# A three-layer chain on one core: the single tile's 256-column groups put side by side into 512-column banks, and three second-layer groups moved into the next phase's first step

## The chip, the cores and the metric

The kernel runs on one core of a Trainium2 chip. Its time is device microseconds (us) of one execution. Engines are called PE (TensorE matmul, with PEld for its weight loads), DVE (VectorE), ACT (ScalarE), POOL (GpSimd) and SP (the engine that issues the DMAs). PSUM, into which PE writes, is used in banks of 128 partitions by 512 float32 columns.

## What is computed

A windowed attention on 4 x 576 tokens (8 heads of 64) gives x, 2304 tokens of 512 numbers. Two layers follow, both cut here to what matters:

```python
# mixture: 8 experts, P is a 2304 x 8 matrix from a softmax and 8 rounds of scaling
for e in range(8):
    out += P[:, e:e+1] * (np.maximum(x @ w1[e], 0) @ w2[e])      # 512 -> 1024 -> 512
# second layer, x is the out of the first
r = np.maximum(x @ w_in, 0)                                      # 512 -> 2048
return (r * r) @ w_out                                           # -> 512
```

## The kernel before

**Tokens.** The 2304 tokens are cut into two pairs of 1024 (tokens 0 to 1023 and 1280 to 2303) and one single tile of 256 (tokens 1024 to 1279). Attention takes the first part of the time; then 80 *steps* follow in four phases, one written after the other (`steps` and `first`, lines 458 to 461): 32 steps of the mixture for the first pair and the single tile (phase 0, steps 0 to 31), 32 for the second pair (phase 1, steps 32 to 63), 8 of the second layer for the first pair and the single tile (phase 2, steps 64 to 71), 8 for the second pair (phase 3, steps 72 to 79). A step takes 256 hidden columns of weights. Every product is done as three float32r matmuls (high by high, high by low part, low by high).

**First layer of a pair** (`l1_pair`, line 536): seven products u1 to u7 of 6 matmuls of 512 columns, a Strassen-like scheme, in PSUM tiles `s` (2 buffers), `xt` (2) and `pt` (1). u4, u5 and u6 all write the one `pt` bank: ACT copies it to `s2` after u4 (line 570) and to `s3` after u5 (line 574), and u5 and u6 wait for these copies. u3 writes again to the bank that ACT copies to `pt` after u1 (line 558).

**First layer of the single tile** (`l1_single`, line 591): two groups (fc 0 and 1) of 12 matmuls of 256 columns, each in half of a bank of its own (tile `mm`, 3 buffers).

**Evacuation** (`evac_g`, line 500): in the mixture from step 3 (`SCALED`) on, DVE makes g = max(z, 0) * p (line 525), ACT rounds it to the high part gh (line 533), DVE takes the low part gl = g - gh (line 511). In the second layer ACT makes max(z, 0) first (line 521). For the single tile p is the tile `ps` of 128 by 256, gh and gl are `sgh` and `sgl`, and each instruction takes 256 columns.

**Second layer** (`l2_units`, line 614): step i does it for the hidden columns of step i-1. The pair has 8 groups of 6 matmuls of 512 columns, which we call l2[0] to l2[7]. The single tile has in the mixture 4 groups of 6 matmuls of 256 columns (called s0 to s3 here), one for each 128 output rows, and in the second layer 2 groups of 512 columns. Each group takes a bank `mm`, and DVE adds the bank to an accumulator in SBUF (line 647). In the last step of a phase's sums the accumulator is stored to DRAM (lines 652 and 655, on SP).

**Order.** It is written out by hand, and each engine's queue is in this order. Within a step: u1 to u4, then l2[0], u5, l2[1], u6, l2[2], u7, then l2[3] to l2[7], then the single tile's second layer, then its first layer (lines 847 to 856). In the first step of a phase (32, 64, 72) all second-layer groups of the step before are run ahead of u1, and u1 to u7 follow each other with none between (lines 842 to 845). In step 64 the two first-layer groups of the single tile stand after u1 and u2 (line 854).

`after(k, f)` (line 484) puts the instructions of f behind the k-th unit from now; a unit is one of the groups above. So all work that is not a matmul has its place by a count of units. `prep_w` (line 123) so splits the next weights: POOL makes sums (lines 144 to 149), ACT rounds (line 131: `w2h` behind unit 1, `blkh` behind 2, `sumh` behind 10), DVE takes the low parts (line 135: `w2l` behind 3, `blkl` behind 5, `suml` behind 12), each no later than the step's last unit (line 858). `new_operands` (line 224) makes the seven operands x of a new phase: 12 pieces behind units 1 to 12 of the step before it and 12 behind units 14 to 25, counted from that step's start, so that the last of them run in the new phase's first step (POOL line 206, ACT line 209, DVE line 212). `narrow` (line 162) turns the second layer's weights from float64 to float32 in four stages; in phase 0 one stage stands behind units 0 and 8 of a step, so every second step has behind unit 8 the stage with three DVE instructions (lines 189 to 196).

```python
            order = l1[:4] if i else l1[2:4]
            for u in l1[4:]:
                order += l2[:1] + [u]
                l2 = l2[1:]
            order += l2 + l2s
```

Of the kernel before, what the change touches and what calls it, by code (L numbers as in the profile page):

```python
# [37 lines left out]
T = 512  # L38
# [9 lines left out]
def tile_kernel(ctx: ExitStack, tc: tile.TileContext, a):  # L48
# [37 lines left out]
    def bank(tag):  # L86
        return psum.tile([128, 512], F32, tag=tag, name=tag, bufs=bufs[tag])
# [163 lines left out]
    def spread(p, e, t0):  # L251
        n = p.shape[-1]
        c0, nch = t0 // 128, n // 128
        src = p_dram[c0:c0 + nch, e:e + 1, :].rearrange("c e n -> e c n")
        nc.sync.dma_start(p.rearrange("p (c n) -> p c n", n=128), src.to_broadcast([128, nch, 128]))
# [7 lines left out]

    def load_ps(e):
        if e < E:
            p = p_t[e] = post[0].tile([128, NSG], F32, tag="ps", name="ps", bufs=1)
            spread(p, e, SINGLE)

# [229 lines left out]
    def evac_g(i, ghi, glo, src, p, k):  # L500
# [21 lines left out]

        def product():
            held["g"] = tmp("g")[:, :n]
            nc.vector.scalar_tensor_tensor(  # L525
                out=held["g"], in0=src, scalar=0.0, in1=held["r"], op0=ALU.max, op1=ALU.mult
            )

        if not moe:
            after(k, square)  # L530
# [58 lines left out]
        return [u1, u2, u3, u4, u5, u6, u7]  # L589

    def l1_single(i):
        def unit(fc):
            if fc == 0:
                g_t[i, 1] = tuple(
                    post[0].tile([128, FC, NSG], F32R, tag=n, name=n, bufs=1) for n in ("sgh", "sgl")
                )
            gh, gl = g_t[i, 1]
            ps = bank("mm")[:, :NSG]
            hi, lo = wset[i % 2]["blk"]
            k = 0  # L600
            for kc in range(KC):
                c = slice((4 * fc + kc) * 128, (4 * fc + kc) * 128 + 128)
                for w, z in ((hi, xs_hi), (hi, xs_lo), (lo, xs_hi)):
                    nc.tensor.matmul(ps, w[:, c], z[:, kc], start=k == 0, stop=k == 3 * KC - 1)  # L604
                    k += 1
            p = p_t[steps[i][1] // SPE] if steps[i][0] and i >= SCALED else None
            evac_g(i, gh[:, fc], gl[:, fc], ps, p, 0)
            s = steps[i][1]
            if fc == FC - 1 and steps[i][0] and s % SPE == SPE - 1:
                after(1, lambda: load_ps(s // SPE + 1))  # L610

        return [lambda fc=fc: unit(fc) for fc in range(FC)]

    def l2_units(i, which):

# [9 lines left out]
        def unit(c, h, w):  # L625
# [20 lines left out]
            else:  # L646
                nc.vector.tensor_tensor(out=dst, in0=ps, in1=dst, op=ALU.add)  # L647
            if i == SCALED - 1:
                p = p_t[0] if which else p_t[0, 0, h // T]
                nc.gpsimd.tensor_tensor(out=dst, in0=dst, in1=p, op=ALU.mult)  # L650
            if last and moe:
                nc.sync.dma_start(y_dram[:, c, t0 + h:t0 + h + w], dst)
            elif last:
                ch = t0 // 128 + c
                nc.sync.dma_start(out[ch * 128:(ch + 1) * 128], dst)

        if moe:
            return [lambda c=c, h=h: unit(c, h, min(T, n)) for h in range(0, n, T) for c in range(KC)]
        return [lambda c=c: unit(c, 0, DM) for c in range(n // 128)]
# [15 lines left out]
    with tc.manual_schedule():  # L675
# [159 lines left out]
        for i in range(len(steps) + 1):  # L835
            l2 = l2_units(i - 1, 0)
            l2s = l2_units(i - 1, 1)
            if i == len(steps):
                for u in l2 + l2s:
                    run(u)  # L840
                break
            if i in first[1:]:
                for u in l2 + l2s:
                    run(u)
                l2, l2s = [], []
            l1 = l1_pair(i) if i else first_units
            order = l1[:4] if i else l1[2:4]
            for u in l1[4:]:
                order += l2[:1] + [u]
                l2 = l2[1:]  # L850
            order += l2 + l2s
            if i == first[2]:
                l1s = l1_single(i)
                order = l1[:1] + l1s[:1] + l1[1:2] + l1s[1:] + l1[2:]
            elif pair_of(i) == 0:
                order += l1_single(i)
            for k, f in prep_w(i):
                after(min(k, len(order) - 1), f)
            if i + 2 in first[1:]:
# [99 lines left out]
```

## Time and profile before

| | us |
|---|---|
| median of 3 runs (2043.14 to 2047.37) | 2044.98 |
| the profiled execution, its own time | 2052.68 |
| its span in the profile | 2050.9 |

The profile is of the one execution of 2052.68 us. All times of rows are microseconds from the start of its span, durations in us unless marked ns. In the timeline and in the chain, successive instructions that are alike are merged (x6 is six of them); `[0.17 <-DVE acc L647]` says that the engine stood idle for 0.17 us before this one and what ended the wait. L635 is line 635 of the kernel. Matmuls overlap: a matmul of 512 columns lasts some 0.39 us in the rows but the next starts 0.23 us after it; so a wait is read from start to start.

### The profile page before, as it was taken

What the parts mean: (1) busy time and instruction counts of PE and PEld (TensorE: products, weight loads), DVE (VectorE), ACT (ScalarE), POOL (GpSimd) and SP (SyncE); (2) the same over time, 40 slices, a digit from 0 to 9 for tenths busy, and PEclk for the clock granted to TensorE, in tenths of its full rate; (3) what the DMA queues carried; (4) which work ended last, traced back from release to release, by engine and by line L of the source; (5) the groups of instructions that cost most, each with busy time, mean ns of one, the idle gap of its engine ahead of it and who ended that gap; (6) DMA issues with size and microseconds to landing.
All of it is one profiled execution on the core that took longest, in us unless ns stands there. A gap on an engine that the chain in (4) does not pass through costs nothing.

```text
span 2050.9 us, 28660 instructions
## 1 busy us (share of the span) xinstructions
PE 2017.1 (98%) x11584; PEld 1663.0 (81%) x11584; DVE 1558.3 (76%) x2435; ACT 720.4 (35%) x1149; POOL 386.6 (19%) x416
## 2 busy tenths in 40 slices
PE   9999999999999999999999999999999999999999
PEld 7778888888888888888888888888888878887887
DVE  4766777777777777778888888888887786678676
ACT  3443222223322232223433333333333344344542
POOL 3522311111011111111311212121211231123120
PEclk8899999999999999999999999999999999999999
DMA  8512121222212121213222322323221231112111
GB/s 279 177 65 61 52 57 57 62 65 62 65 50 61 56 61 47 70 57 98 103 93 87 87 85 71 97 78 98 82 86 59 75 111 42 39 54 103 62 42 52
DMA packets 71509, 159.35 MB, mean 78 GB/s; under 512 B 6336, under 2 KB 33104, under 8 KB 71376
## 3 DMA queue, kind: packets, MB, share of 16 engines
q1 hardware_dynamic: 71376, 157.52, 23.8%
q8 instruction: 91, 1.49, 0.3%
q14 instruction: 42, 0.34, 0.1%
HBM read 137.49 MB, written 20.00 MB: 77 GB/s over the span
## 4 chain that ended last, share of the span: by engine, by line
PE 87%; DVE 10%; ACT 2%; issue 1%; POOL 0%; ACTq 0%; DVEq 0%; POOLq 0%
PE mm L635 42%; PE pt L477 16%; PE s L477 10%; PE xt L477 9%; PE mm L604 5%; DVE acc L647 3%; PE xt L349 2%; DVE gl L511 2%; DVE g L525 1%; DVE suml L135 1%; PE mm L752 1%; PE s L297 1%; PE pt L334 1%; DVE x_lo L212 1%; DVE s L584 1%
## 5 line engine op out<-in xcount | busy, mean ns | idle before, releaser
L647 DVE TENSOR_TENSOR acc<-mm,acc 128x512 f32<-128x512 f32 x746 | 473.2, 642 | 188.4 <-PE mm L635 184.4
L635 PE MATMUL mm<-gl,w2h 128*128 128x512 f32 x1024 | 403.3, 394 | 0.0
L635 PE MATMUL mm<-gh,w2h 128*128 128x512 f32 x1024 | 402.3, 393 | 0.8 <-DVE acc L647 0.7
L635 PE MATMUL mm<-gh,w2l 128*128 128x512 f32 x1024 | 402.8, 393 | 0.0
L533 ACT CAST gh<-g 128x512 fp32r<-128x512 f32 x308 | 191.5, 622 | 592.8 <-DVE g L525 592.6
L144 POOL TENSOR_TENSOR sums<-raw 128x256 f32<-128x256 f32 x80 | 66.2, 827 | 1466.7 <-DVE suml L135 1423.8
L635 PEld LDWEIGHTS mm<-gh,w2h 128*128 128x128 f32 x1024 | 192.4, 188 | 46.8 <-DVE acc L647 1.6
L635 PEld LDWEIGHTS mm<-gl,w2h 128*128 128x128 f32 x1024 | 192.3, 188 | 43.9
L635 PEld LDWEIGHTS mm<-gh,w2l 128*128 128x128 f32 x1024 | 192.3, 188 | 43.7
L511 DVE TENSOR_TENSOR gl<-g,gh 128x512 fp32r<-128x512 f32 x308 | 223.8, 731 | 0.9 <-ACT gh L533 0.9
L525 DVE SCALAR_TENSOR_TENSOR g<-s,pp 128x512 f32<-128x512 f32 x183 | 128.8, 704 | 111.6 <-PE s L477 109.4
L477 PE MATMUL pt<-x_hi,sumh 128*128 128x512 f32 x320 | 126.4, 395 | 3.7 <-ACT s L570 3.7
L477 PE MATMUL s<-x_hi,blkh 128*128 128x512 f32 x320 | 126.3, 395 | 1.0 <-ACT pt L558 1.0
L477 PE MATMUL xt<-x_hi,sumh 128*128 128x512 f32 x320 | 126.6, 396 | 0.0
L477 PE MATMUL xt<-x_lo,sumh 128*128 128x512 f32 x320 | 126.0, 394 | 0.0
L477 PE MATMUL pt<-x_lo,sumh 128*128 128x512 f32 x320 | 125.9, 393 | 0.0
L477 PE MATMUL xt<-x_hi,suml 128*128 128x512 f32 x320 | 125.9, 393 | 0.0
L477 PE MATMUL pt<-x_hi,suml 128*128 128x512 f32 x320 | 125.8, 393 | 0.0
L477 PE MATMUL s<-x_lo,blkh 128*128 128x512 f32 x320 | 125.8, 393 | 0.0
L477 PE MATMUL s<-x_hi,blkl 128*128 128x512 f32 x320 | 125.5, 392 | 0.0
L135 DVE TENSOR_TENSOR w2l<-raw,w2h 128x1024 fp32r<-128x1024 f32 x80 | 100.7, 1259 | 14.9 <-ACT w2h L131 14.9
L533 ACT CAST sgh<-g 128x256 fp32r<-128x256 f32 x74 | 29.9, 406 | 219.0 <-DVE g L525 219.0
(151 smaller groups left out, 3970.3 us busy)
## 6 DMA issues: line engine op xcount, KB each, us to landing
raw<-in_w SPq DMA_DIRECT2D x128, 512.0 KB, 3.5
raw<-w SPq DMA_DIRECT2D x32, 512.0 KB, 3.4
v<-in_v SPq DMA_DIRECT2D x24, 384.0 KB, 3.9
pp<-p_dram SPq DMA_DIRECT2D x32, 256.0 KB, 5.6
xb<-in_w_in SPq DMA_DIRECT2D x16, 512.0 KB, 4.7
w<-xb SPq DMA_DIRECT2D x32, 256.0 KB, 2.3
xb<-in_w_out SPq DMA_DIRECT2D x16, 512.0 KB, 4.7
k<-in_k SPq DMA_DIRECT2D x24, 224.0 KB, 4.6
```

The lines of the kernel that those rows point to most:

```text
L135: nc.vector.tensor_tensor(out=w[1], in0=src, in1=w[0].bitcast(F32), op=ALU.subtract)
L144: tt(out=c(sums, 0), in0=c(raw1, 2), in1=c(raw1, 3), op=ALU.add)
L212: return lambda: nc.vector.tensor_tensor(out=x_lo[:, k, j], in0=z, in1=x_hi[:, k, j].bitcast(F32), op=ALU.subtract)
L297: nc.tensor.matmul(ps[QB * head:QB * head + QB, 2 * (g % 3) + g // 3, :], qt[rows, pr, g * QB:g * QB + QB], kt[rows, pr, g * QB:g * QB + K ...
L349: nc.tensor.matmul(xt[D * h:D * h + D, pr, c * QB:c * QB + QB], vt[keys, c, head * D:head * D + D], pt[keys, c * 128 + head * QB:c * 128 + ...
L477: nc.tensor.matmul(ps, w[:, c], z[:, x, j], start=start and k == 0, stop=stop and k == 5, skip_group_check=True)
L511: nc.vector.tensor_tensor(out=glo, in0=z, in1=ghi.bitcast(F32), op=ALU.subtract)
L525: nc.vector.scalar_tensor_tensor(out=held["g"], in0=src, scalar=0.0, in1=held["r"], op0=ALU.max, op1=ALU.mult)
L533: after(k + 1, lambda: nc.scalar.copy(ghi, held["g"]))
L604: nc.tensor.matmul(ps, w[:, c], z[:, kc], start=k == 0, stop=k == 3 * KC - 1)
L635: nc.tensor.matmul(ps, lhsT, rhs, start=k == 0, stop=k == 3 * FC - 1)
L647: nc.vector.tensor_tensor(out=dst, in0=ps, in1=dst, op=ALU.add)
```

## The change

The single tile's first layer becomes one unit for steps from 3 on: both groups of 12 matmuls go into the two halves of one bank, and evacuation takes 512 columns at a time (the tile `ps` gets a middle dimension, so that it can be read twice over). In the mixture its second layer becomes two units (`unit_wide`) of 12 matmuls from step 4 on, each with two groups in one bank, one addition of 512 columns and in the last step one store. A step of phase 0 has then 18 units instead of 21, one of phase 2 18 instead of 19. In the first step of a phase the last three second-layer groups of the pair are kept back and stand before u5, u6 and u7 as in other steps; the other five and the single tile's run ahead as before. In step 64 the single tile's first-layer unit stands after u1.

```diff
--- before.py
+++ after.py
@@ -263,8 +263,8 @@
 
     def load_ps(e):
         if e < E:
-            p = p_t[e] = post[0].tile([128, NSG], F32, tag="ps", name="ps", bufs=1)
-            spread(p, e, SINGLE)
+            p = p_t[e] = post[0].tile([128, 1, NSG], F32, tag="ps", name="ps", bufs=1)
+            spread(p[:, 0, :], e, SINGLE)
 
 
 
@@ -522,9 +522,12 @@
 
         def product():
             held["g"] = tmp("g")[:, :n]
-            nc.vector.scalar_tensor_tensor(
-                out=held["g"], in0=src, scalar=0.0, in1=held["r"], op0=ALU.max, op1=ALU.mult
-            )
+            o, z, r = held["g"], src, held["r"]
+            if len(r.shape) == 3:
+                k = n // NSG
+                o, z = (y.rearrange("p (k n) -> p k n", k=k) for y in (o, z))
+                r = r.to_broadcast([128, k, NSG]) if k > 1 else r
+            nc.vector.scalar_tensor_tensor(out=o, in0=z, scalar=0.0, in1=r, op0=ALU.max, op1=ALU.mult)
 
         if not moe:
             after(k, square)
@@ -589,27 +592,34 @@
         return [u1, u2, u3, u4, u5, u6, u7]
 
     def l1_single(i):
-        def unit(fc):
-            if fc == 0:
+        def unit(fcs):
+
+            if fcs[0] == 0:
                 g_t[i, 1] = tuple(
                     post[0].tile([128, FC, NSG], F32R, tag=n, name=n, bufs=1) for n in ("sgh", "sgl")
                 )
             gh, gl = g_t[i, 1]
-            ps = bank("mm")[:, :NSG]
+            ps = bank("mm")[:, :len(fcs) * NSG]
             hi, lo = wset[i % 2]["blk"]
-            k = 0
-            for kc in range(KC):
-                c = slice((4 * fc + kc) * 128, (4 * fc + kc) * 128 + 128)
-                for w, z in ((hi, xs_hi), (hi, xs_lo), (lo, xs_hi)):
-                    nc.tensor.matmul(ps, w[:, c], z[:, kc], start=k == 0, stop=k == 3 * KC - 1)
-                    k += 1
+            for n, fc in enumerate(fcs):
+                k = 0
+                for kc in range(KC):
+                    c = slice((4 * fc + kc) * 128, (4 * fc + kc) * 128 + 128)
+                    for w, z in ((hi, xs_hi), (hi, xs_lo), (lo, xs_hi)):
+                        nc.tensor.matmul(
+                            ps[:, n * NSG:n * NSG + NSG], w[:, c], z[:, kc], start=k == 0, stop=k == 3 * KC - 1
+                        )
+                        k += 1
             p = p_t[steps[i][1] // SPE] if steps[i][0] and i >= SCALED else None
-            evac_g(i, gh[:, fc], gl[:, fc], ps, p, 0)
+            gh, gl = (g[:, fcs[0]:fcs[-1] + 1].rearrange("p f n -> p (f n)") for g in (gh, gl))
+            evac_g(i, gh, gl, ps, p, 0)
             s = steps[i][1]
-            if fc == FC - 1 and steps[i][0] and s % SPE == SPE - 1:
+            if fcs[-1] == FC - 1 and steps[i][0] and s % SPE == SPE - 1:
                 after(1, lambda: load_ps(s // SPE + 1))
 
-        return [lambda fc=fc: unit(fc) for fc in range(FC)]
+        if i >= SCALED:
+            return [lambda: unit(list(range(FC)))]
+        return [lambda fc=fc: unit([fc]) for fc in range(FC)]
 
     def l2_units(i, which):
 
@@ -646,7 +656,7 @@
             else:
                 nc.vector.tensor_tensor(out=dst, in0=ps, in1=dst, op=ALU.add)
             if i == SCALED - 1:
-                p = p_t[0] if which else p_t[0, 0, h // T]
+                p = p_t[0][:, 0, :] if which else p_t[0, 0, h // T]
                 nc.gpsimd.tensor_tensor(out=dst, in0=dst, in1=p, op=ALU.mult)
             if last and moe:
                 nc.sync.dma_start(y_dram[:, c, t0 + h:t0 + h + w], dst)
@@ -654,6 +664,28 @@
                 ch = t0 // 128 + c
                 nc.sync.dma_start(out[ch * 128:(ch + 1) * 128], dst)
 
+        def unit_wide(c):
+
+            ps = bank("mm")
+            for m in range(2):
+                k = 0
+                for fc in range(FC):
+                    for g, wt in ((gh, whi), (gl, whi), (gh, wlo)):
+                        nc.tensor.matmul(
+                            ps[:, m * NSG:m * NSG + NSG],
+                            wt[:, fc, (c + m) * 128:(c + m) * 128 + 128],
+                            g[:, fc],
+                            start=k == 0,
+                            stop=k == 3 * FC - 1,
+                        )
+                        k += 1
+            dst = acc[1][:, c * NSG:c * NSG + 2 * NSG]
+            nc.vector.tensor_tensor(out=dst, in0=ps, in1=dst, op=ALU.add)
+            if last:
+                nc.sync.dma_start(y_dram[:, c:c + 2, t0:t0 + NSG], dst.rearrange("p (c n) -> p c n", c=2))
+
+        if moe and which and i >= SCALED:
+            return [lambda c=c: unit_wide(c) for c in (0, 2)]
         if moe:
             return [lambda c=c, h=h: unit(c, h, min(T, n)) for h in range(0, n, T) for c in range(KC)]
         return [lambda c=c: unit(c, 0, DM) for c in range(n // 128)]
@@ -839,21 +871,21 @@
                 for u in l2 + l2s:
                     run(u)
                 break
+            ahead = []
             if i in first[1:]:
-                for u in l2 + l2s:
-                    run(u)
-                l2, l2s = [], []
+                ahead, l2, l2s = l2[:-3] + l2s, l2[-3:], []
             l1 = l1_pair(i) if i else first_units
             order = l1[:4] if i else l1[2:4]
+            l1s = l1_single(i) if pair_of(i) == 0 else []
+            if i == first[2]:
+                order = l1[:1] + l1s + l1[1:4]
+                l1s = []
             for u in l1[4:]:
                 order += l2[:1] + [u]
                 l2 = l2[1:]
-            order += l2 + l2s
-            if i == first[2]:
-                l1s = l1_single(i)
-                order = l1[:1] + l1s[:1] + l1[1:2] + l1s[1:] + l1[2:]
-            elif pair_of(i) == 0:
-                order += l1_single(i)
+            order += l2 + l2s + l1s
+            for u in ahead:
+                run(u)
             for k, f in prep_w(i):
                 after(min(k, len(order) - 1), f)
             if i + 2 in first[1:]:
```

## Rows read from the trace of the kernel before

**Rows 1.** The page, part 1: busy time of each engine, share of the span, instructions.
```profile
PE 2017.1 (98%) x11584; PEld 1663.0 (81%) x11584; DVE 1558.3 (76%) x2435; ACT 720.4 (35%) x1149; POOL 386.6 (19%) x416
```
**Rows 2.** Waits of PE, whole span: who waited for whom, us, times, longest.
```profile
PE mm L635 <- DVE acc L647: 11.3, 31, 1.4
```
**Rows 3.** Chain in order of time, first-layer groups of the single tile: start, us, what.
```profile
865.65 2.88 PE mm L604 x24
...
893.24 2.83 PE mm L604 x24
...
919.90 2.88 PE mm L604 x24
...
946.41 2.83 PE mm L604 x24
```
**Rows 4.** Timeline of PE in one step's tail: start, us, engine, line, operation.
```profile
346.58 0.28 PE L635 MATMUL mm<-sgh,w2h 128*128 128x256 f32 x1
...
347.62 0.39 PE L635 MATMUL mm<-sgh,w2h 128*128 128x256 f32 x1 [0.17 <-DVE acc L647]
...
348.98 0.38 PE L635 MATMUL mm<-sgh,w2h 128*128 128x256 f32 x1 [0.38 <-DVE acc L647]
...
350.51 0.28 PE L604 MATMUL mm<-xs_hi,blkh 128*128 128x256 f32 x1
```
**Rows 5.** Timeline of DVE in the same tail.
```profile
346.88 0.69 DVE L647 TENSOR_TENSOR acc<-mm,acc 128x512 f32<-128x512 f32 x1
...
348.25 1.34 DVE L647 TENSOR_TENSOR acc<-mm,acc 128x512 f32<-128x512 f32 x3
```
**Rows 6.** Timeline of PE in the tail of the next step.
```profile
375.46 0.28 PE L635 MATMUL mm<-sgh,w2l 128*128 128x256 f32 x1
375.69 0.38 PE L635 MATMUL mm<-sgh,w2h 128*128 128x256 f32 x1
```
**Rows 7.** Timeline of PE in the tail of step 31.
```profile
970.15 0.38 PE L635 MATMUL mm<-sgh,w2h 128*128 128x256 f32 x1
...
972.48 0.38 PE L635 MATMUL mm<-sgh,w2h 128*128 128x256 f32 x1 [1.37 <-DVE acc L647]
...
975.16 0.28 PE L604 MATMUL mm<-xs_hi,blkh 128*128 128x256 f32 x1
```
**Rows 8.** Groups by form, DVE's evacuations: xcount | busy us, mean ns | idle before.
```profile
L647 DVE TENSOR_TENSOR acc<-mm,acc 128x512 f32<-128x512 f32 x622 | 426.0, 687 | 167.7 <-PE mm L635 163.8
...
L647 DVE TENSOR_TENSOR acc<-mm,acc 128x256 f32<-128x256 f32 x124 | 49.6, 417 | 20.6 <-PE mm L635 20.6
```
**Rows 9.** Timeline of PE in step 32: u4 to u5 and u5 to u6.
```profile
997.19 0.40 PE L477 MATMUL pt<-x_hi,suml 128*128 128x512 f32 x1
998.26 0.50 PE L477 MATMUL pt<-x_hi,sumh 128*128 128x512 f32 x1 [0.67 <-ACT s L570]
998.59 0.40 PE L477 MATMUL pt<-x_lo,sumh 128*128 128x512 f32 x1
...
1000.60 0.50 PE L477 MATMUL pt<-x_hi,blkh 128*128 128x512 f32 x1 [0.68 <-ACT s L574]
```
**Rows 10.** Waits of PE from 1646 to 1690 (into step 64, and 65): us, times, longest.
```profile
PE pt L477 <- ACT s L570: 1.1, 2, 0.7
PE mm L635 <- DVE acc L647: 0.7, 1, 0.7
...
PE s L477 <- ACT pt L558: 0.5, 1, 0.5
```
**Rows 11.** Timeline of DVE at the end of step 64.
```profile
1676.68 1.23 DVE L135 TENSOR_TENSOR suml<-sums,sumh 128x1024 fp32r<-128x1024 f32 x1 [2.65 <-ACT sumh L131]
1677.83 0.68 DVE L525 SCALAR_TENSOR_TENSOR g<-pt,r 128x512 f32<-128x512 f32 x1
```
**Rows 12.** Timeline of POOL as step 64 begins.
```profile
1661.90 1.19 POOL L144 TENSOR_TENSOR sums<-raw 128x256 f32<-128x256 f32 x1
```
**Rows 13.** Timeline of PE: four transposes into one bank, side by side.
```profile
82.41 0.60 PE L392 MATMUL mm<-ident,lt 128*128 128x128 f32 x4
```

## The prediction

> **What bounds the kernel now.** I began with the busy times: PE is busy for 98% of the span, DVE for 76% [rows 1]. The change takes away no matmul, so its worth lies in PE's 2% of waits and in nothing else; shorter work on DVE or ACT counts only where PE waits for it. The waits of PE name the largest such sum: 11.3 us in 31 waits of second-layer groups for DVE's addition that frees their bank [rows 2]. That view leaves out short waits, so I measured them as lengths of steps. In the chain the single tile's first-layer groups come once a step of phase 0, and their distances are 27.59, 26.66 and 26.51 [rows 3]. The reader is to see that the first and the last are steps of one kind (2.83 for their 24 matmuls, so the same weight buffer) and differ by 1.08; the short one, step 30, is the only one of its kind without weight narrowing.
>
> The timeline of PE shows where the 1.08 sits [rows 4]. s0 begins at 346.58 and the first-layer groups at 350.51: 3.93 for 24 matmuls of 256 columns, which take 24 x 0.119 = 2.86 unhindered (2.83 to 2.88 for 24 [rows 3]). s1 is late by 0.33 and s2 by 0.54, and each loses another 0.10 after its wait. Three banks go round: s0 takes the bank of l2[5], s1 that of l2[6], s2 that of l2[7]. DVE adds l2[6] only at 346.88 and l2[7], the first of the merged three, only at 348.25 [rows 5]; it is behind because of the narrowing. Groups of 0.71 use up three banks faster than DVE, behind as it is, returns them.
>
> The second place is the first step of phases 1, 2 and 3. From the last matmul of u4 to the first of u5 there are 1.07 in step 32 instead of 0.23, and the next start comes 0.33 later instead of 0.23; u5 to u6 the same [rows 9]. PE waits there for ACT to empty the one `pt` bank, which in other steps an l2 group covers.
>
> **The change part by part.** *Joined second layer of the tile, phase 0.* w0 (s0 and s1) starts at 346.58 and ends at 348.01. w1 needs the bank of l2[6], free at 346.88 + 0.69 = 347.57: no wait. The first-layer unit needs the bank of l2[7], free at 348.25 + 0.68 = 348.93, and comes at 346.58 + 2.86 = 349.44: no wait. The margins are 0.44 and 0.51, and DVE's work up to there doesn't change. So the step falls to 26.51, and there are 12 such steps (6, 8, to 28): 12 x 1.08 = 13.0. The 13 steps of the other kind (5, 7, to 29) are 26.66; in their tails s2 is late by 0.11 (0.23 from 375.46 to 375.69 where 0.12 is the rule) [rows 6], and about 0.10 follows it, as behind the waits of step 32 [rows 9]. Joined, s2 is the second half of w1's place and needs no bank: 13 x 0.21 = 2.7, with 0 and 2.7 as ends, and I take the upper one since the same margins of 0.4 apply. Step 31 is further behind: from s0 at 970.15 to the first layer at 975.16 are 5.01, of which 2.15 are waits, most of it before s1 [rows 7]. There l2[6]'s bank comes at 972.48, 2.33 after s0; w1 wants it after 1.43. So w1 waits 0.90 plus 0.10, the rest goes: 1.15. Step 3 still runs the old groups of step 2 and gains nothing.
>
> *Joined evacuation.* Two additions of 417 ns become one of 687 [rows 8]; the product, the rounding and the low part halve in number likewise. A pair of additions saves 0.15 so, which has no value by itself. The price is order: DVE's product now stands until both first-layer groups are done, idle for up to 2.9 where it was idle twice for about 1. Queued behind it are the low part and, in narrowing steps, two DVE instructions; nobody waits for them before the next step's tail, and DVE has 24% to spare [rows 1]. Reading `ps` twice over in one instruction: no row shows this on DVE; between nothing and a doubling of 0.69, hidden either way by the same slack, so 0. The load of `ps` stands one unit behind the last product as before. The tile's two stores instead of four, once: 0.
>
> *Three groups kept back.* Steps 32, 64 and 72 lose their two waits on `pt`: (0.84 + 0.10) x 2 = 1.9 each [rows 9], as an l2 group of 1.4 (6 x 0.23) is longer than the 0.94 lost. In steps 64 and 65 more waits stand: one of 0.5 before u3 for ACT's copy, a second one for L570 of 0.4 [rows 10]. Scaled by the idle time named and the loss of step 32 (0.67 and 0.94) [rows 9] these are some 0.77 and 0.67 to 0.73; I take 1.5. Their cause: `suml`, pushed to the last unit of a short step, waited 2.65 for ACT, and the product that empties `pt` came after it [rows 11]. With three more units in the step that product stands ahead of `suml`, so both go. Steps 72 and 73 repeat the pattern of 64 and 65. Gains: 1.9 + 3.4 + 3.4 = 8.7. The kept groups' additions stand on DVE among u5 to u7 as in every other step; in step 32 their stores stand on SP between the two weight loads, whose data is wanted a step later: 0.
>
> *Pieces of the new operands.* They keep their unit numbers, but in step 64 only five groups run ahead instead of eight, so the last pieces come behind u1 to u4 and the first kept group, among the products that read them. The latest: a POOL subtraction, which now stands behind the four POOL sums of the step (1.19 the first [rows 12], so some 4.7), then its rounding on ACT, and behind that ACT's copy to `s2`, for which u5 waits. I get u5 held by 0 to 0.6 and take 0.3. In steps 32 and 72 the tile's two units run ahead as well, and only one piece is left behind u1: 0.
>
> **Sum.** 13.0 + 2.7 + 1.15 + 8.7 - 0.3 = 25.2; the three kept groups run beside matmuls that follow each other more slowly (the two weight buffers differ by 2% [rows 3]), some 0.1 a start, and one of the 26.66 steps may keep a wait: I take 24.5. The profiled execution goes from 2052.68 to 2028.2. It lies 7.7 above the median of the runs shown, for a reason that the trace doesn't show; no term of the sum hangs on it, so the median becomes 2044.98 - 24.5 = 2020.5.
>
> **The rivals.**
> *The starts give nothing.* ACT or DVE, more crowded there by the kept groups, holds u5 and u6 as long as now: 2044.98 - 16.9 + 0.7 (the same deductions) = 2028.8. For it speaks that ACT is the late one; against it, that the same order has no wait in any other step of phases 1 to 3.
> *The tails give half.* DVE falls behind by 0.5 more than it did, w1 and the first layer wait again: 13.0 halves, 2027.
> *The tail's waits stay whole.* DVE has slack, so its number of instructions may not be what holds PE; it begins on a joined bank 0.7 later, and the waits move with it. Then only the starts count: 2037. Against it: the two banks that PE waits for are those of l2[6] and l2[7], which DVE adds before any joined bank. The Trainium skill, Perfetto Trace Analysis, section Optimizing Scalar/DVE Operations, says that where these engines aren't saturated but hold others up, breaking instructions up may help; and its section Optimizing Tensor Performance wants independent groups to rotate through banks, so that evacuation overlaps. Both speak against this change. By them the time would be these 2037; the trace agrees with them only in that PE waits for a bank in the round [rows 4, 5].
> *Slower: PE empties between two groups in one bank.* If the second group's start has to wait until the first one's results are out, each switch costs the rest of the last matmul (0.28 - 0.12) and at worst a first one that nothing overlaps, as long as those behind a wait (0.38 - 0.12) [rows 4]: 0.42. There are 29 x 2 switches in joined second-layer groups and 29 + 8 in first-layer ones: 95 x 0.42 = 40, and 2020.5 + 40 = 2060. It decides from 0.26 a switch on. Against it: four transposes into neighbouring columns of one bank take 0.60 in all [rows 13], 0.11 from start to start, though each is a group of its own.
> *It does nothing*, as waits are kept by something not seen: 2045.
>
> **How the numbers follow.** The forecast gets 0.74, the starts 0.07, the half 0.07, the whole waits 0.05, the switch 0.04, nothing 0.03. Below the forecast lie waits that I left standing (0.7 before step 64 [rows 10], 1.0 in step 31, others in steps 3 and 71, some 5 in all): 2015. Above, the starts and the half reach to 2029, with 2 for a median's own spread: 2031. 2037, 2045 and 2060 stay out, 0.12 in all. Faster by over 0.2% (4.1 us, about what a measurement of this kernel can tell from no change): 0.93; within: 0.03; slower: 0.04.
>
> **What would show it.** Right: in phase 0 the distances of the first-layer groups alternate near 26.5 with none over 26.7; PE's waits for L647 fall from 31 to under 10, step 31 keeping one of about 0.7; the `pt` waits at the three starts are gone. Wrong: waits of the first-layer unit for L647; a gap of more than 0.15 at the 7th or 13th matmul of a joined bank; a wait of u4 or u5 in step 64 for DVE's or ACT's operand pieces over 0.6.

## The result and the profile after

The changed kernel takes 2021.12 us (median of 4 runs, 2019.44 to 2025.04) where the kernel before, beside it, took 2046.17 (4 runs, 2043.14 to 2048.59). The ratio is 0.9873, 95% interval 0.9856 to 0.9890: faster, and 0.6 us from the forecast of 2020.5. The profiled execution of the changed kernel took 2019.84, with a span of 2018.1.

The busy times on the first page are those of before [rows 1] with PE at 99%: fewer DVE and ACT instructions, the same 11584 matmuls.

```profile
PE 1995.4 (99%) x11584; PEld 1653.2 (82%) x11584; DVE 1544.1 (77%) x2303; ACT 712.5 (35%) x1104; POOL 388.1 (19%) x416
```

The waits of PE after the start of the steps (from 120 us on). In the new kernel the pair's second layer is L645, its addition L657, the tile's joined second layer L674 with its addition L683, and the tile's first layer L609. The 31 waits of 11.3 us for L647 [rows 2] have become six of 3.7 in all, and no wait for ACT's copies of `pt` is in the list (the line for L435 is a wait of the softmax work in step 0, 1.0 before):

```profile
PE mm L645 <- DVE acc L657: 3.0, 5, 1.1
PE mm L435 <- DVE scs L429: 0.9, 1, 0.9
PE mm L674 <- DVE acc L657: 0.7, 1, 0.7
```

The chain, the tile's first layer in phase 0. Its distances are 26.53, 26.48 and 26.52, where they were 27.59, 26.66 and 26.51 [rows 3], in the same three steps. The 24 matmuls take 2.83 to 2.88 as before, now with a change of group inside a bank after the twelfth:

```profile
843.00 2.88 PE mm L609 x24
...
869.53 2.83 PE mm L609 x24
...
896.01 2.88 PE mm L609 x24
...
922.53 2.83 PE mm L609 x24
```

The timeline of PE in the tail that rows 4 show of the kernel before: from the first joined second-layer matmul to the first layer 2.87 instead of 3.93, without a wait.

```profile
336.43 0.28 PE L674 MATMUL mm<-sgh,w2h 128*128 128x256 f32 x1
...
337.86 0.28 PE L674 MATMUL mm<-sgh,w2h 128*128 128x256 f32 x1
...
339.30 0.28 PE L609 MATMUL mm<-xs_hi,blkh 128*128 128x256 f32 x1
```

The timeline of DVE there. l2[6] is added 0.30 and l2[7] 1.67 after PE began the tail (336.43). Before they were added at 0.30 and 1.67 too [rows 4, 5]: DVE frees the two banks no earlier, PE merely asks for them later. The price is in the last line, where the product waits for both first-layer groups:

```profile
336.73 0.68 DVE L657 TENSOR_TENSOR acc<-mm,acc 128x512 f32<-128x512 f32 x1
...
338.10 0.68 DVE L657 TENSOR_TENSOR acc<-mm,acc 128x512 f32<-128x512 f32 x1
338.70 1.49 DVE L683 TENSOR_TENSOR acc<-mm,acc 128x512 f32<-128x512 f32 x2
342.33 0.69 DVE L530 SCALAR_TENSOR_TENSOR g<-mm,ps 128x512 f32<-128x512 f32 x1 [2.14 <-PE mm L609]
```

Step 31 keeps one wait and comes to its first layer 3.81 after its first joined group, where it took 5.01 [rows 7]:

```profile
946.28 0.39 PE L674 MATMUL mm<-sgh,w2h 128*128 128x256 f32 x1
...
948.62 0.38 PE L674 MATMUL mm<-sgh,w2h 128*128 128x256 f32 x1 [0.68 <-DVE acc L657]
...
950.09 0.28 PE L609 MATMUL mm<-xs_hi,blkh 128*128 128x256 f32 x1
```

Step 32, u4 to u6 (answers to rows 9): the kept groups stand between them and every start follows the last one by 0.23 or 0.24.

```profile
968.03 0.40 PE L477 MATMUL pt<-x_hi,suml 128*128 128x512 f32 x1
968.27 0.39 PE L645 MATMUL mm<-gh,w2h 128*128 128x512 f32 x1
...
969.41 0.39 PE L645 MATMUL mm<-gh,w2l 128*128 128x512 f32 x1
969.64 0.40 PE L477 MATMUL pt<-x_hi,sumh 128*128 128x512 f32 x1
```

**Where the time went.** In the timeline of PE I took the start of u1 in every step, and from it the length of stretches. What runs ahead of u1 in a phase's first step counts to the step before it, so each of the three starts lies in a stretch that begins one step early. "Rest" is from step 0's u1 to the end of the last instruction of a compute engine; the span ends 3.4 later in both kernels.

| kernel | step 0 starts | steps 4-30 | 31-32 | 33-62 | 63-65 | 66-70 | 71-73 | rest |
|---|---|---|---|---|---|---|---|---|
| before | 117.45 | 730.78 | 54.42 | 625.20 | 75.42 | 131.59 | 75.67 | 1930.0 |
| changed | 108.86 | 715.56 | 51.41 | 625.25 | 72.40 | 131.59 | 72.72 | 1905.8 |
| difference | -8.6 | -15.22 | -3.01 | 0.05 | -3.02 | 0 | -2.95 | -24.2 |

So the change is worth 24.2 from step 0 on. The 8.6 ahead of it are no work of the change: they are attention, whose code is the same. The two profiled executions are 2052.68 - 2019.84 = 32.8 apart, 24.2 and 8.6, while the medians are 25.1 apart. The granted clock of that part differs between the two. These are windows of PE of before and then of the changed kernel: us, busy time and count, PEclk (1.00 is 2.4 GHz, 0.50 is 1.2), DMA share, GB/s.

```profile
37.00:52.00 15.00, 15.00 (x253) 0.54 0.56 185
61.00:72.00 11.00, 10.96 (x204) 0.54 0.74 249
```
```profile
37.00:52.00 15.00, 14.10 (x405) 1.00 0.68 203
61.00:72.00 11.00, 10.33 (x291) 1.00 0.75 228
```

The execution of before ran most of both windows at the lower level, the other at the upper one. The runs of the kernel before that were not profiled go the same way: beside the first experiments the three at 2052.15 to 2052.62 had a mean granted clock of 0.994, the six at 2043.53 to 2044.14 one of 0.999. The twelve profiled executions of this study start step 0 anywhere from 108.9 to 117.5. So the column "rest" separates kernels more sharply than the medians, and I use it below. It comes from one profiled execution of each kernel; how far it can be trusted show two stretches that no edit aims at: in all twelve kernels steps 66 to 70 take 131.59, and steps 33 to 62 take 625.17 to 625.50.

### The profile page after: what moved, and what is told of

It reads as the page before. It is cut to its first block, busy times and chain, and to the rows that moved or that the text cites. A ratio compares the mean times of both kernels' runs of the same rounds, so it can differ in the third digit from the quotient of the medians.

```text
span 2018.1 us, 28458 instructions
## 1 busy us (share of the span) xinstructions
PE 1995.4 (99%) x11584; PEld 1653.2 (82%) x11584; DVE 1544.1 (77%) x2303; ACT 712.5 (35%) x1104; POOL 388.1 (19%) x416
## 3 DMA queue, kind: packets, MB, share of 16 engines
q1 hardware_dynamic: 71344, 157.52, 24.2%
## 4 chain that ended last, share of the span: by engine, by line
PE 93%; DVE 5%; ACT 1%; issue 0%; DMA 0%; SPq 0%; POOL 0%; ACTq 0%; DVEq 0%; POOLq 0%
PE mm L645 43%; PE pt L477 16%; PE s L477 11%; PE xt L477 10%; PE mm L609 6%; PE mm L674 4%; PE xt L349 1%; DVE acc L657 1%; DVE g L530 1%; DVE x_lo L212 1%; DVE suml L135 1%; PE pt L334 1%; PE mm L784 0%; PE s L297 0%; DVE gl L511 0%
## 5 line engine op out<-in xcount | busy, mean ns | idle before, releaser
L657 DVE TENSOR_TENSOR acc<-mm,acc 128x512 f32<-128x512 f32 (+1 forms) x630 | 429.0, 683 | 173.1 <-PE mm L645 168.9
L645 PE MATMUL mm<-gl,w2h 128*128 128x512 f32 x1024 | 403.2, 394 | 0.0
L645 PE MATMUL mm<-gh,w2h 128*128 128x512 f32 x1024 | 402.3, 393 | 0.8 <-DVE acc L657 0.7
L645 PE MATMUL mm<-gh,w2l 128*128 128x512 f32 x1024 | 402.8, 393 | 0.0
L645 PEld LDWEIGHTS mm<-gh,w2h 128*128 128x128 f32 x1024 | 192.4, 188 | 46.8 <-DVE acc L657 1.6
L645 PEld LDWEIGHTS mm<-gl,w2h 128*128 128x128 f32 x1024 | 192.3, 188 | 44.0
L645 PEld LDWEIGHTS mm<-gh,w2l 128*128 128x128 f32 x1024 | 192.3, 188 | 43.8
L530 DVE SCALAR_TENSOR_TENSOR g<-s,pp 128x512 f32<-128x512 f32 x183 | 128.8, 704 | 95.8 <-PE s L477 93.6
L536 ACT CAST sgh<-g 128x512 fp32r<-128x512 f32 x37 | 23.0, 621 | 224.9 <-DVE g L530 224.9
```

The costliest lines, as they stand in the source:

```text
L530: nc.vector.scalar_tensor_tensor(out=o, in0=z, scalar=0.0, in1=r, op0=ALU.max, op1=ALU.mult)
L536: after(k + 1, lambda: nc.scalar.copy(ghi, held["g"]))
L645: nc.tensor.matmul(ps, lhsT, rhs, start=k == 0, stop=k == 3 * FC - 1)
```

## The experiments

Ratios are to the kernel before, run beside on the same chip; its medians there were 2045.05 (19 runs, beside the kernels with a_), 2046.79 (7, b_) and 2046.22 (7, c_). Each kernel has 4 runs, a_keep_only and a_l1join_only 10, c_keep_sums 1. Lengths are from the timelines, as above. The diffs show the lines that matter, not each whole edit.

| kernel | time | ratio, 95% | step 0 starts | 4-30 | 31-32 | 63-65 | 71-73 | rest |
|---|---|---|---|---|---|---|---|---|
| a_tail_only | 2028.61 | 0.9916 (0.9897-0.9934) | 109.68 | 715.56 | 53.26 | 75.40 | 75.69 | 1913.5 |
| a_l2join_only | 2028.22 | 0.9917 (0.9897-0.9936) | 112.37 | 715.56 | 53.26 | 75.36 | 75.68 | 1913.6 |
| a_l1join_only | 2046.81 | 1.0002 (0.9985-1.0018) | 112.02 | 730.92 | 54.43 | 75.39 | 75.68 | 1929.9 |
| b_swap_only | 2027.78 | 0.9907 (0.9891-0.9922) | 109.49 | 715.56 | 53.93 | 75.40 | 75.68 | 1912.9 |
| b_split_evac | 2021.94 | 0.9876 (0.9862-0.9891) | 110.30 | 715.56 | 51.43 | 72.39 | 73.34 | 1906.4 |
| a_keep_only | 2040.32 | 0.9979 (0.9965-0.9993) | 113.49 | 730.71 | 53.05 | 73.87 | 72.73 | 1924.2 |
| b_keep2 | 2026.77 | 0.9902 (0.9887-0.9918) | 111.13 | 715.56 | 51.64 | 73.92 | 74.24 | 1909.3 |
| b_suml_wide | 2021.74 | 0.9875 (0.9858-0.9893) | 115.96 | 715.56 | 50.83 | 73.02 | 71.46 | 1903.1 |
| c_best | 2018.04 | 0.9864 (0.9845-0.9884) | 111.00 | 715.56 | 50.79 | 71.16 | 71.46 | 1901.3 |
| c_keep_sums | 2040.94 | one run | 112.73 | 730.62 | 53.02 | 73.11 | 72.74 | 1923.1 |

### The tail alone, and its two halves

The changed kernel with no group kept back (a_tail_only):

```diff
-                ahead, l2, l2s = l2[:-3] + l2s, l2[-3:], []
+                ahead, l2, l2s = l2 + l2s, [], []
```

> The joined groups alone; all second-layer groups of a phase's last step run ahead again. Bank theory (PE waits because three banks are used up faster than DVE returns them): the tails gain what the change's trace shows, 12 x 1.07 + 13 x 0.18 + 1.1 = 16.3, so about 2030 beside 2046 for the kernel before; the waits on pt in the first steps of phases 1 to 3 stay, 1.9 in each. If the two parts need each other (the starts gain only because DVE is lighter, or the other way round), the two single kernels together gain clearly less than 25.

Only the second layer joined (a_l2join_only: `unit_wide` added to the kernel before, its first layer left in two units):

```diff
+        if moe and which and i >= SCALED:
+            return [lambda c=c: unit_wide(c) for c in (0, 2)]
```

> Only the tile's second-layer groups of the mixture are joined; its first layer keeps two banks and two evacuations, and nothing is kept back. Bank theory: the first of the two first-layer groups comes to the bank of l2[7] at the same moment as the joined one, so this is the whole gain of the tails: 2030, as with both joined. Rival (DVE's number of instructions sets the wait): 58 of the 161 instructions that DVE loses in phase 0 are lost here, so about a third of the 16: 2040.

Only the first layer and its evacuation joined (a_l1join_only: the changed kernel without that return, and no group kept back):

```diff
-        if moe and which and i >= SCALED:
-            return [lambda c=c: unit_wide(c) for c in (0, 2)]
```

> Only the tile's first-layer groups are joined, with their evacuation of 512 columns; the second layer keeps s0 to s3. Bank theory: s1 and s2 want the same banks at the same moments, so nothing is gained: 2046, and the distances of the first-layer groups keep their 27.59 and 26.66. Rival (DVE's number of instructions): two thirds of the 16, 2035.

Joined second-layer groups give the whole -15.22 of steps 4 to 30 and the 1.2 of step 31 (54.42 - 53.26); in the tails of phase 0 the joined first layer gives nothing, alone or beside them. In the waits of PE the 31 waits stand unchanged with the first layer joined, and fall to those of the changed kernel with the second layer joined. First the one, then the other:

```profile
PE mm L645 <- DVE acc L657: 11.2, 31, 1.4
```
```profile
PE mm L635 <- DVE acc L647: 3.1, 5, 1.1
...
PE mm L664 <- DVE acc L647: 0.7, 1, 0.7
```

The joined first layer halves the number of DVE's evacuations of it too, and that is worth nothing there: the number of instructions was not the cause. (The "58 of the 161" of the expectation is a miscount: DVE has 2435 instructions before, 2303 in the changed kernel, 2377 with only the second layer joined and 2361 with only the first, so 58 and 74 of 132. By its number the two kernels would have shared the gain about evenly.)

### Nothing joined, only the order turned

The kernel before, with the tile's first-layer groups ahead of its second-layer groups in the mixture from step 3 on (b_swap_only; DVE's products move with the groups, their rounding and low parts moved behind the second layer that still reads `sgh` and `sgl`):

```diff
-            order += l2 + l2s
+            order += l2
+            if steps[i][0] and pair_of(i) == 0 and i >= SCALED:
+                order += l1_single(i)
+            order += l2s
```

> The kernel before with one thing changed in phase 0 from step 3 on: the tile's two first-layer groups stand ahead of its four second-layer groups (the rounding of their results is put behind the second layer, which still reads the old ones). No group is joined and DVE has as many instructions as before. Bank theory: the groups that come to the banks of l2[6] and l2[7] are now 1.42 long instead of 0.71, so the waits go as with joined banks: 2030. Rival (joining itself, fewer and larger instructions): no gain, 2046.

Steps 4 to 30 take the same 715.56, to the hundredth. The three banks are those of l2[5], l2[6] and l2[7] in both cases; a first-layer group of 12 matmuls lasts as long as a joined unit of two second-layer groups, so the second and the third bank are again asked for 1.43 and 2.86 after the tail's start instead of 0.71 and 1.43. The timeline of PE in the tail of the same step as above shows 48 matmuls in 5.71 with no wait, though no bank holds two groups:

```profile
335.52 0.28 PE L610 MATMUL mm<-xs_hi,blkh 128*128 128x256 f32 x1
...
338.35 0.28 PE L662 MATMUL mm<-sgh,w2h 128*128 128x256 f32 x1
...
341.23 0.40 PE L477 MATMUL s<-x_hi,blkh 128*128 128x512 f32 x1
```

DVE's additions of l2[6] and l2[7] stand there again 0.30 and 1.67 after the tail's start (335.52):

```profile
335.82 0.68 DVE L674 TENSOR_TENSOR acc<-mm,acc 128x512 f32<-128x512 f32 x1
...
337.19 0.68 DVE L674 TENSOR_TENSOR acc<-mm,acc 128x512 f32<-128x512 f32 x1
```

So what counts is when PE asks for the second and the third bank, not how full a bank is. From step 0 on this version is 17.1 below the kernel before, a little more than the joined tail's 16.5: steps 0 to 3 take 99.25 instead of 100.84, since step 3 has the new order already. Step 31 is the exception, where the swap is worth 0.49 and not 1.16: it keeps the wait for l2[6] (0.6), and in the pair's groups that follow, PE waits another 0.5 for an addition (L674), which stands on DVE behind the tile's two low parts (2.40 together there).

### The evacuation cut in two again

The changed kernel with each joined bank emptied by two instructions of 256 columns (b_split_evac):

```diff
-            nc.vector.tensor_tensor(out=dst, in0=ps, in1=dst, op=ALU.add)
+            for m in range(2):
+                h = slice(m * NSG, m * NSG + NSG)
+                nc.vector.tensor_tensor(out=dst[:, h], in0=ps[:, h], in1=dst[:, h], op=ALU.add)
```
```diff
-            evac_g(i, gh, gl, ps, p, 0)
+            for n, fc in enumerate(fcs):
+                evac_g(i, gh[:, fc], gl[:, fc], ps[:, n * NSG:n * NSG + NSG], p, 0)
```

> The changed kernel, but every joined bank is emptied in two halves: two additions, two products, two roundings, two low parts of 256 columns. Bank theory: 2021, as the changed kernel, since the two banks waited for are emptied before any joined one. Rival (DVE's number of instructions): the gain of the tails is lost, about 2037.

No difference in the tails of phase 0; steps 71 to 73 get 0.6 longer, all of it in step 71, and the cause stays open. The Trainium skill, Perfetto Trace Analysis, section Optimizing Scalar/DVE Operations, says that breaking instructions up may help where an engine isn't saturated but holds others up. In the tails here it neither helps nor hurts (715.56 in both kernels): PE waited for additions that stood ahead of the ones that are broken up.

### The kept groups alone

The kernel before with three groups kept back and nothing joined (a_keep_only):

```diff
-                for u in l2 + l2s:
-                    run(u)
-                l2, l2s = [], []
+                ahead, l2, l2s = l2[:-3] + l2s, l2[-3:], []
```

> The three kept groups alone; the tile's groups in half banks as before. Theory of the parts adding up: 1.9 in step 32 and about 3.2 each in steps 64/65 and 72/73, 8.3 in all: about 2038. If the kept groups only help with the lighter tail: 2044 to 2046.

Slower than expected by 2; from step 0 on it gains 5.8 where 8.3 was expected. Steps 71 to 73 gained 2.94, as in the changed kernel; steps 31 and 32 gained 1.37, where the starts' part of the changed kernel is 1.8 (why is open); and 63 to 65 gained 1.55 instead of 3.02. The waits of PE there name ACT's copy behind u4 (L570), for 1.2 (1620 to 1690):

```profile
PE pt L477 <- ACT s L570: 1.2, 1, 1.2
```

The timelines of step 64 suggest why. This kernel's POOL: the third and fourth sum take 1.20 and 1.60, and the last operand subtraction (the last line) starts 5.88 after the one before it:

```profile
1653.91 1.68 POOL L206 TENSOR_TENSOR xb<-xb 128x512 f32<-128x512 f32 x1 [1.64 <-DVE x_lo L212]
...
1656.94 1.20 POOL L148 TENSOR_TENSOR sums<-sums,raw 128x256 f32<-128x256 f32 x1
1658.22 1.60 POOL L149 TENSOR_TENSOR sums<-raw,sums 128x256 f32<-128x256 f32 x1
1659.79 1.74 POOL L206 TENSOR_TENSOR xb<-xb 128x512 f32<-128x512 f32 x1
```

The changed kernel's POOL in the same place: no sum over 0.76, and 4.57 between the two.

```profile
1632.38 1.69 POOL L206 TENSOR_TENSOR xb<-xb 128x512 f32<-128x512 f32 x1 [1.64 <-DVE x_lo L212]
...
1635.41 0.76 POOL L148 TENSOR_TENSOR sums<-sums,raw 128x256 f32<-128x256 f32 x1
1636.24 0.75 POOL L149 TENSOR_TENSOR sums<-raw,sums 128x256 f32<-128x256 f32 x1
1636.95 1.75 POOL L206 TENSOR_TENSOR xb<-xb 128x512 f32<-128x512 f32 x1
```

The difference is DVE. In this kernel it starts its low parts beside the second half of the sums; in the changed one it stands idle for 3.03, until 1635.93, waiting for the joined first layer, while the first three sums start. DVE's rows, first of this kernel, then of the changed one:

```profile
1656.35 1.20 DVE L212 TENSOR_TENSOR x_lo<-xb,x_hi 128x512 fp32r<-128x512 f32 x1
1657.46 1.76 DVE L135 TENSOR_TENSOR w2l<-raw,w2h 128x1024 fp32r<-128x1024 f32 x1
```
```profile
1635.93 0.69 DVE L530 SCALAR_TENSOR_TENSOR g<-mm,r 128x512 f32<-128x512 f32 x1 [3.03 <-ACT r L521]
1636.54 1.00 DVE L212 TENSOR_TENSOR x_lo<-xb,x_hi 128x512 fp32r<-128x512 f32 x1
```

By these rows the joined first layer does give something after all, in one step: its late product keeps DVE out of POOL's way. No run shows it apart, since none has the kept groups and only one of the two joinings. It is also where the parts fail to add up: the joined tail alone gives 16.5 and the kept groups alone 5.8, together 22.3 of 24.2; of the missing 1.9, 1.5 are in steps 63 to 65 and 0.5 in steps 31 and 32.

### Two groups kept instead of three

The changed kernel with two groups kept back (b_keep2):

```diff
-                ahead, l2, l2s = l2[:-3] + l2s, l2[-3:], []
+                ahead, l2, l2s = l2[:-2] + l2s, l2[-2:], []
```

> The changed kernel with two groups kept back instead of three (ahead of u5 and u6, none ahead of u7). The waits on pt need only these two, so they stay away. If the late waits in steps 65 and 73 come from the place of suml in a short step: with one unit fewer suml is put ahead of the product that empties pt again, and a wait for ACT's copy of 0.5 to 0.8 returns in step 65 and step 73, some 1 to 1.5 in all: 2022.5. If they came from ACT being crowded, two kept groups do as well as three: 2021.

Slower than either expectation. Steps 63 to 65 and 71 to 73 each give back 1.52, by one wait each of 1.3 for ACT's copy that follows u1 (L561 here, L558 before):

```profile
PE s L477 <- ACT pt L561: 2.5, 2, 1.3
```

In kind it is the wait for that copy in [rows 10] and its cause in [rows 11]: with one unit less, `suml` stands ahead of the product that empties `pt` again. DVE's rows at the end of step 64:

```profile
1651.13 1.23 DVE L135 TENSOR_TENSOR suml<-sums,sumh 128x1024 fp32r<-128x1024 f32 x1 [2.12 <-ACT sumh L131]
...
1652.99 0.69 DVE L530 SCALAR_TENSOR_TENSOR g<-pt,r 128x512 f32<-128x512 f32 x1
```

The size that was expected, 1 to 1.5 in all, is half of the 3.04 that came.

### `suml` moved, and the second layer joined two steps earlier

The changed kernel with two more moves (b_suml_wide). In steps 31, 63 and 71 `suml` goes behind unit 17 instead of 12, past the tail's additions; in steps 32, 64 and 72 `sumh` and `suml` come three or four units ahead of the step's end; and the tile's second layer is joined two steps earlier, for the tails of steps 2 and 3.

```diff
+                if i + 1 in first[1:] and k == 12:
+                    k = 17
+                elif i in first[1:] and k in (10, 12):
+                    k = len(order) - (4 if k == 10 else 3)
```
```diff
-        if moe and which and i >= SCALED:
+        if moe and which and i >= 1:
```

> The changed kernel with two more moves. suml is put behind unit 17 in the last steps of phases 0 to 2 (31, 63, 71), so that DVE adds l2[6] and l2[7] first, and three units before the end in the first steps of phases 1 to 3, where the weight load of the next step's u2 waits for it in the changed kernel (0.3 in steps 65 and 73). And the tile's second layer is joined from step 2 on. If the waits left over (about 1.1 in step 31, 1.1 ahead of step 64, 1.6 in step 71, 1.6 in step 3, 0.6 in steps 65 and 73, 6 in all) are of the same kind, 4 to 6 go: 2015 to 2017. If DVE's backlog is whole and only moves, 2020 to 2022.

From step 0 on it is 2.7 below the changed kernel, where 4 to 6 were expected: 1.44 in steps 0 to 3 (nearly all in step 3), 0.58 in 31 and 32, 1.26 in 71 to 73. But 63 to 65 got 0.62 longer, and the median isn't lower; its profiled execution came to step 0 at 115.96, 7.1 later than the changed kernel's. The rows of ACT in step 64 show the loss: the last rounding of an operand piece waits 2.42 for POOL, and the copy for which u5 waits (1.7 in the waits of PE) stands behind it.

```profile
1645.36 0.62 ACT L209 CAST x_hi<-xb 128x512 fp32r<-128x512 f32 x1 [2.42 <-POOL xb L206]
1645.88 0.58 ACT L573 COPY s<-pt 128x512 f32<-128x512 f32 x1
```

It is the queue that the prediction put down with 0 to 0.6, now at 1.7.

### The four sums moved behind the last operand piece

The kernel above (c_best), and the one with only the kept groups (c_keep_sums), each with POOL's sums in step 64 three units later:

```diff
-            for k, f in prep_w(i):
+            for n, (k, f) in enumerate(prep_w(i)):
+                if i == first[2] and n < 2:
+                    k += 3
```

> The kernel with the wide product of step 2 and suml earlier, and in step 64 the four POOL sums stand behind units 3 and 4 instead of 0 and 1, so that the last operand subtraction no longer stands behind them. Theory (that subtraction held ACT's rounding, ACT's copy to s2 and so u5 by 1.68): the stretch of steps 63 to 65 falls from 73.02 us to some 71.3, all other stretches stay, and the time from the first step's start to the end is 1901 to 1902. Rival (ACT's queue itself is full there): 63 to 65 stays at 73. For the median: 2.7 + 1.7 = 4.4 below the changed kernel by the traces, so 2017, if the attention's part is as long as in that kernel's runs; up to 2021 if it is not.

> The kernel that only keeps three groups back (nothing joined), with the same move of POOL's four sums in step 64 behind units 3 and 4. Theory (the 1.2 us for which u5 waited there came from those sums ahead of the last operand subtraction): the stretch 63 to 65 falls from 73.87 to 72.3 to 72.7, the rest stays (1922.5 to 1923 from the first step's start to the end). Rival (order of the single tile's two half groups among u1 to u3 holds it): no change, 73.9.

In the first, 63 to 65 fell from 73.02 to 71.16 and the rest from 1903.1 to 1901.3, as the theory had it (71.3, and 1901 to 1902). Its waits of PE after 120 us are down to these, of which the first two are in step 0:

```profile
PE mm L435 <- DVE scs L429: 0.9, 1, 0.9
PE pt L477 <- ACT s L577: 0.4, 1, 0.4
PE mm L645 <- DVE acc L657: 0.2, 1, 0.2
```

It is the fastest version of the study, 2018.04 (2015.38 to 2022.78, 4 runs), ratio 0.9864 (0.9845 to 0.9884). From step 0 on it is 4.5 below the changed kernel; the intervals of the two ratios overlap, so that part is shown by the stretches only.

In the second, 63 to 65 fell by 0.76 only, from 73.87 to 73.11; 72.3 to 72.7 was expected. The wait for L570 fell from 1.2 to 0.4. So the sums were the larger part of that wait, and something else holds the copy for the remaining 0.4: in ACT's rows the copy (1661.02) stands behind a max of the pair's first layer (1660.23) that by the profile waited 2.20 for DVE's low part of the tile.

## Why the prediction was right

**The tails of phase 0.** Forecast 15.7 for steps 4 to 30, measured 15.22. The twelve steps with the late narrowing went from 27.59 to 26.52, 1.07 each where 1.08 was forecast, and the margins of 0.44 and 0.51 were enough, since DVE's additions stood where they had stood. (One reading was inexact: step 30 has the three narrowing instructions too, but 1.7 to 2.9 after its u1 instead of 14.0 to 15.1, so that they are done long before its tail.) The thirteen others gave 15.22 - 12 x 1.07 = 2.4, or 0.18 each where 0.21 was taken. The swap shows the reason itself: the time between two demands of a bank. Reading `ps` twice over, priced between nothing and a doubling, took nothing: the joined product lasts 0.69 (L530, 342.33), the pair's product at 334.40 0.68.

**Step 31.** Forecast 1.15, measured 5.01 - 3.81 = 1.20, with one wait left: the second joined unit starts 2.34 after the first instead of 1.43, so it is 0.91 late (0.90 forecast; the 0.68 in its row is PE's idle time alone).

**The starts.** Step 32 gave 3.01 - 1.20 = 1.8 (forecast 1.9). For 64 and 65 I forecast 3.4 - 0.3 and 3.02 came; for 72 and 73 3.4, and 2.95 came. Both sizes hide one miss. In steps 65 and 73 a wait stands that I had not seen. The timeline of PE in step 65 shows it, at the third matmul of u2, and DVE's row says what it waits for, `suml`, which starts behind two products now:

```profile
1649.21 0.39 PE L477 MATMUL xt<-x_lo,sumh 128*128 128x512 f32 x1
1649.67 0.50 PE L477 MATMUL xt<-x_hi,suml 128*128 128x512 f32 x1
1650.01 0.39 PE L477 MATMUL xt<-x_hi,sumh 128*128 128x512 f32 x1
```
```profile
1648.40 1.22 DVE L135 TENSOR_TENSOR suml<-sums,sumh 128x1024 fp32r<-128x1024 f32 x1
```

The two starts are 0.46 and 0.34 apart instead of 0.23 twice: 0.34 lost, in each of the two places. The prediction's step "the product stands ahead of `suml`, so both go" was right about the wait that went and did not ask who waits for `suml` when it comes later. With that 0.34 added back the gains are 3.36 and 3.29, near the 3.4. **The operand pieces** in step 64 cost nothing where 0.3 was taken. I had priced POOL's sums at the 1.19 of the first [rows 12]; they took 0.74 to 0.76, for the reason that the kept groups alone show.

**The sum.** 24.5 was taken, 24.2 measured from step 0 on. That it comes so near is in part luck. The parts added up to 25.2 and came to 24.2: 0.5 less in the tails and 0.45 less in steps 71 to 73. The 0.7 that was taken off had other reasons, one of which did not come (no 26.66 step kept a wait; all thirteen are at 26.48). Between the medians lie 25.05; as step 0 begins up to 8.6 earlier or later from one profiled execution to the next, the 0.6 by which the forecast median was missed is closer than the reasoning could promise.

**The rivals.** That PE empties at each change of group inside a bank falls by the 2.83 and 2.88 of the chain. That the waits stay whole, because DVE holds PE by the number or the size of its instructions, falls by the evacuation cut in two (no change) and by the joined first layer alone (no gain). The starts gave nearly what they were to give, and the tail gave all, not half.

**The 7.7 us** by which the profiled execution of before lay above its median I called something that the trace doesn't show. That was wrong: the trace shows a granted clock of 0.54 in two stretches of the attention part, and the other runs of that kernel that took 2052 have the lower mean clock too. No term hung on it.

## What to carry to other kernels

Where PE waits for a bank, set the times at which it asks for each buffer of the ring against the times at which the evacuating engine returns them. A run of short groups asks for the buffers faster than an engine that is behind with other work returns them; in steps 4 to 30 here, putting longer groups in front was as good as joining short ones (715.56 in both), in step 31 it was not (0.49 against 1.16). An instruction that is moved later in a queue must be followed to its own readers too, and a wait that a change opens by accident (DVE idle while POOL works) may carry part of the gain, as it seems to here.

## What the runs showed of the hardware

**DVE and POOL slow each other.** In step 64 a DVE subtraction of 512 columns with both inputs in SBUF takes 0.68 where POOL stands idle and up to 1.26 beside POOL's sums and subtractions (kernel before); a sum of 256 columns takes 0.74 where DVE stands idle and up to 1.60 beside such work (a_keep_only; 1.72 in c_best). In these rows the one that starts first keeps its time: in a_keep_only the second sum starts at 1656.24 and takes 0.75, the subtraction that starts at 1656.35 takes 1.20, and the third sum, begun at 1656.94 while that subtraction runs, takes 1.20. The joined first layer's product, which reads PSUM and one operand in SBUF, keeps its 0.69 beside POOL's sums (1635.93). The Trainium skill, SBUF — State Buffer, section Who interferes with whom, says that a DVE instruction with two SBUF inputs contends with a GpSimd instruction that reads SBUF, and that one with at most one SBUF input, outside the two-port modes, doesn't; these rows agree.

**The granted clock in the first 72 us differs between executions of one and the same code.** In the stretch from 24 to 37 us PE was busy for 11.73 of 13.00 in the execution of before and for 11.57 in the other, both at 0.98 to 0.99; then the one fell to 1.2 GHz for most of the next 15 us and the other stayed at 2.4. Why is not settled. Step 0 begins up to 8.6 us later or earlier with it, which is more than several of the edits here are worth.
